# Odd tokens of two batches in one tile, and reciprocals on 128 partitions by way of DRAM, in an attention and gated-MLP kernel for one Trainium2 core

## Chip, core and metric

The kernel runs on one core of a Trainium2 chip. The metric is the device time of one execution in microseconds. Five engines matter: TensorE (PE, matmuls), VectorE (DVE), ScalarE (ACT), GpSimd (POOL) and SyncE (SP), whose queue issues nearly all DMAs.

## What is computed

Four batches of 12 heads, 448 tokens and 64 values a head go through capped attention; the result, 448 tokens by 768, goes through a gated MLP with a residual. In short, from the reference:

```python
scores = cap * np.tanh(scale * np.matmul(q, k.transpose(0, 1, 3, 2)) / cap)
attn = np.exp(scores - np.max(scores, axis=-1, keepdims=True))
attn = attn / (np.sum(attn, axis=-1, keepdims=True) + 1e-09)
x = np.matmul(attn, v)                      # heads side by side: (4, 448, 768)
h = gelu_tanh(x @ w_in)                     # (4, 448, 1024)
u, v = h[..., :512], h[..., 512:]
v_n = (v - mu) / np.sqrt(var + 1e-06) * g_ln
v_s = np.einsum('ts,bsd->btd', w_sg, v_n) + b_sg[None, :, None]
out = x + (u * v_s) @ w_out
```

All inputs are fp32 (`w_in` and `w_out` are float64 words that the kernel decodes itself). To keep the precision, every dense product is made of three matmuls: a value is split into a high part and a rest (both fp32r), and high x high, high x low and low x high are summed in PSUM.

## The kernel before

**Attention.** A batch is 6 pairs of heads, in 3 groups of two pairs. A group has 7 units (L294 to L301): three blocks of 128 keys for each pair, and one unit that holds the odd 64 keys of both pairs. So there are 84 units. A unit is a score product in one of two PSUM tiles `sc` (L533, or L541 for the odd keys, L547 for the very first), a Tanh (L602) and an Exp (L604) of 128 x 896 on ACT into one of six tiles `p`, a product with v into `ps` (L561, L571) and, alone or after a sum on DVE (L621), a product with ones (L478) that adds the row sums into the PSUM bank `den`. DVE or ACT split q and k into `hl` beforehand and copy `ps` into the tiles `x` behind.

**Reciprocals and normalisation.** `recip` (L628) waits for the last L478 of a batch, copies half of `den` (on DVE or ACT), adds the other half and the guard (L631), takes the reciprocals on 64 partitions of 448 (L634) and writes them to DRAM in two DMAs (L637). `norm` (L660) then fetches, for each pair, its two rows spread over 128 partitions (L664, two tiles `n`), multiplies (L667) and splits into `xh` and `xl` (copy, L354). The odd 64 tokens of `xl` also go into columns 448 to 511 of `xh` (L672).

**Gated part.** `gated(b)` has four stages on PE: `hv` (L705, v = x w_in, token tiles of 128 and one of the odd 64 tokens whose other 64 columns hold the low parts), `hu` (L750, u), `vsg` (L767, the product with `w_sg`) and `outp` (L788). Each `hv` and `hu` tile goes through a gelu: ACT (L686), DVE (L688), ACT (L691), DVE (L693). `hv` tiles are then normalised: L724 to L726 on DVE, a power on POOL (L729), L737, and a split. The odd tile has a further copy and addition first (L719, L720), on 64 partitions.

**Order.** Nothing is issued in the order of the text. `Plan` (L128) collects operations with their costs and keys, and `run` (L164) places them on the five queues by a model of the engines: of what is ready first, the lowest key. The keys come from a table of numbers (L23 to L45: `ATT`, `GATED`, `RECIP` and others). The queues themselves are then fixed: each engine works in its order, and an instruction that waits holds all behind it. The odd tile's matmuls in `hv` before are these:

```python
terms = ((0, 0), (0, 1), (1, 0)) if t < FC else ((0, 0), (0, 1))
for c in range(KD):
    ...
            rhs=win[w][:, c, HF:], start=(c == 0 and k == 0),
```

Of the kernel before, what the change touches and what calls it, by code (L numbers as in the profile page):

```python
# [28 lines left out]
SHARED = {'act': 206.9, 'dve': 108.5}
SUMS = (0, 0, 1, 0, 1, 1, 1, 1, 1, 1, 1, 1)  # L30
RETIRE = (12, 9, 12, 12, 12, 0)
IN_V = (95.8, 10.2)
IN_U = (189.1, 37.0)
OUT_W = (-35.4, 5.8)
SG_W = (583.9, 11.2)
FETCH_W = 59.61
FETCH_G = 58.41
SPLIT = 0.0
SG_FETCH = (47.2, 64.6)
GELU = 157.26  # L40
NORM = 236.9
RECIP = 414.62
VAL = 30.18
DEN = 24.2
DEC_AHEAD = 49.6  # L45
# [833 lines left out]
```

## Time and profile before

| | |
|---|---|
| median of 3 runs | 399.18 us (398.41 to 399.54) |
| the profiled execution, its own time | 397.81 us |
| its span, first to last instruction | 396.0 us |
| PE busy | 381.1 us, 96% |
| DVE busy | 301.6 us, 76% |
| ACT busy | 240.1 us, 61% |
| POOL busy | 45.8 us, 12% |
| TensorE clock granted | 1.00 throughout |

Busy time is the time in which at least one instruction of the engine runs. The profiled execution has 1.81 us outside its span and lies 1.37 us under the median. Shares over the whole span hide that DVE and ACT work mostly in the first 280 us: a table by stretches tells more.

### The profile page before, as it was taken

The page shows a single profiled execution, that of the slowest core. Times are in us where ns is not written, and L with a number is a line of the kernel's source. Part 1 is how long each engine was busy: PE and PEld are TensorE (multiplying, and loading weights), DVE is VectorE, ACT ScalarE, POOL GpSimd, SP SyncE. Part 2 cuts the span into 40 slices and gives each one's busy share as a digit, 9 for nine tenths or more (in the row PEclk, how much of TensorE's full clock was granted, in tenths as well). Part 3 has the DMA queues.
Part 4 walks back from the last instruction along what each step waited for, and adds up shares of the span by engine and source line. Part 5 has one row for each costly group of instructions (what it writes and reads, how often), then busy time and mean ns, then how long its engine had stood idle before and what let it go on. Part 6 is the DMA issues. An engine that isn't in the chain of part 4 may idle for free.

```text
span 396.0 us, 5622 instructions
## 1 busy us (share of the span) xinstructions
PE 381.1 (96%) x2118; PEld 254.3 (64%) x2118; DVE 301.6 (76%) x527; ACT 240.1 (61%) x318; POOL 45.8 (12%) x40
## 2 busy tenths in 40 slices
PE   4999999999999999799999999999999999999996
PEld 1343434465458664273564789998488999889995
DVE  3799999899987898888989278575387876387551
ACT  5999999799794489957968744340323532143210
POOL 0244111014231110113110011000001000010000
PEclk9999999999999999999999999999999999999999
DMA  7995454716042136617162000003012002100012
GB/s 250 293 333 160 145 165 117 239 44 187 7 141 71 48 91 188 215 50 228 46 204 102 25 0 0 2 0 116 26 55 93 2 0 94 46 0 2 1 46 93
DMA packets 23690, 38.85 MB, mean 98 GB/s; under 512 B 3248, under 2 KB 21104, under 8 KB 23664
## 3 DMA queue, kind: packets, MB, share of 16 engines
q1 hardware_dynamic: 23520, 38.39, 30.6%
q8 instruction: 16, 0.26, 0.3%
q10 hardware_dynamic: 144, 0.11, 0.1%
q14 instruction: 10, 0.08, 0.1%
HBM read 32.64 MB, written 5.85 MB: 97 GB/s over the span
## 4 chain that ended last, share of the span: by engine, by line
PE 73%; DVE 9%; DMA 8%; POOL 3%; issue 3%; ACT 1%; SPq 1%; DVEq 0%; ACTq 0%; POOLq 0%
PE ps L788 9%; PE ps L561 9%; PE ps L750 8%; PE sc L533 8%; PE ps L705 7%; PE ps L767 7%; PE sc L750 6%; DMA n<-spread 6%; PE sc L788 5%; PE den L478 4%; PE sc L705 4%; PE sc L541 2%; PE sc L767 2%; POOL sm L729 2%; DMA stage<-in_w_out_dram 2%
## 5 line engine op out<-in xcount | busy, mean ns | idle before, releaser
L602 ACT ACTIVATE p<-sc,qsc 128x896 f32<-128x896 f32 x84 | 81.4, 1007 | 17.0 <-PE sc L533 12.2
L604 ACT ACTIVATE p<-p,cap_sb 128x896 f32<-128x896 f32 x84 | 84.2, 1046 | 0.2
L561 PE MATMUL ps<-p,v 128*64 128x448 f32 x288 | 61.2, 553 | 0.6 <-ACT p L604 0.5
L533 PEld LDWEIGHTS sc<-hl 64*128 64x128 f32 x426 | 36.5, 186 | 35.8 <-ACT p L602 21.5
L533 PE MATMUL sc<-hl 64*128 64x448 f32 x426 | 56.9, 390 | 2.2 <-ACT p L602 2.1
L420 POOL TENSOR_TENSOR stage<-stage 128x512 int32<-128x512 int32 (+1 forms) x20 | 32.3, 1618 | 148.2 <-DVE stage L415 143.1
L621 DVE TENSOR_TENSOR p<-p,p 128x896 f32<-128x896 f32 x36 | 39.0, 1089 | 7.1 <-PE ps L561 3.8
L705 PE MATMUL ps<-win,rg 128*128 128x512 f32 x176 | 44.1, 397 | 0.2 <-DVE rg L354 0.2
L788 PE MATMUL ps<-rg,wout 128*128 128x448 f32 x188 | 42.5, 369 | 0.1
L561 PEld LDWEIGHTS ps<-p,v 128*64 128x64 f32 x288 | 17.8, 137 | 37.1 <-issue 25.5
L705 PEld LDWEIGHTS ps<-win,rg 128*128 128x128 f32 x176 | 32.8, 187 | 9.0 <-DVE rg L354 1.4
L788 PEld LDWEIGHTS ps<-rg,wout 128*128 128x128 f32 x188 | 34.9, 188 | 4.6 <-issue 0.6
L750 PE MATMUL ps<-rg,win 128*128 128x448 f32 x166 | 37.1, 367 | 0.7 <-DVE win L354 0.7
L750 PEld LDWEIGHTS ps<-rg,win 128*128 128x128 f32 x166 | 31.1, 188 | 3.9 <-DVE win L354 1.1
L729 POOL TENSOR_TENSOR sm<-sm,pw 128x1 f32<-128x1 f32 (+1 forms) x16 | 13.3, 832 | 166.4 <-DVE sm L726 166.4
L686 ACT ACTIVATE t<-ps 128x448 f32<-128x448 f32 (+1 forms) x18 | 10.2, 566 | 35.2 <-PE ps L705 22.4
L691 ACT ACTIVATE t<-t 128x448 f32<-128x448 f32 (+2 forms) x32 | 19.4, 605 | 18.9 <-DVE t L688 18.9
L767 PE MATMUL ps<-wsg,rg 128*128 128x448 f32 x129 | 29.3, 369 | 0.0
L478 PE MATMUL den<-p,ones_sb 128*32 128x448 f32 x192 | 26.1, 550 | 2.1 <-DVE p L621 2.1
L354 DVE TENSOR_TENSOR hl<-raw,hl 128x896 fp32r<-128x896 f32 (+1 forms) x25 | 27.6, 1107 | 0.6 <-ACT hl L326 0.5
L767 PEld LDWEIGHTS ps<-wsg,rg 128*128 128x128 f32 x129 | 24.1, 188 | 3.6 <-DVE rg L354 0.7
L326 ACT ACTIVATE rg<-u 128x448 fp32r<-128x448 f32 x14 | 8.1, 579 | 27.1 <-DVE u L776 27.1
(106 smaller groups left out, 506.2 us busy)
## 6 DMA issues: line engine op xcount, KB each, us to landing
stage<-in_w_in_dram SPq DMA_DIRECT2D x12, 512.0 KB
raw<-in_q_dram SPq DMA_DIRECT2D x24, 224.0 KB
raw<-in_k_dram SPq DMA_DIRECT2D x24, 224.0 KB
n<-spread SPq DMA_DIRECT2D x24, 224.0 KB
...
```

The lines of the kernel that those rows point to most:

```text
L354: op("dve", c_tt(n), lambda: nc.vector.tensor_tensor(out=out(), in0=a(), in1=b(), op=ALU.subtract), rd=rd, wr=wr, key=key, fast=True)
L420: nc.gpsimd.tensor_tensor(out=a.bitcast(I32), in0=a.bitcast(I32), in1=hi, op=ALU.add)
L478: nc.tensor.matmul(out=den.t[32 * j:32 * j + 32, :S], lhsT=ones_sb[:, kind, NP - 1 - kind - p:NP + 31 - kind - p], rhs=src.t[:, h, :], sta ...
L533: nc.tensor.matmul(out=sc.t[:, h, :S], lhsT=hl[s].t[rows, w, 1, 128 * c - 128:128 * c], rhs=hl[s].t[rows, m, 0], start=(k == 0), stop=(k = ...
L561: nc.tensor.matmul(out=pav[s].t[64 * h:64 * h + 64, :S], lhsT=v[s].t[:, 128 * (c - 1) + 64 * h:128 * (c - 1) + 64 * h + 64], rhs=p.t[:, h, ...
L602: op("act", c_act(2 * S, True, True), lambda p=p, sc=sc: nc.scalar.activation(out=p.t, in_=sc.t[:, :, :S], func=ACTF.Tanh, scale=qsc), rd= ...
L604: op("act", c_act(2 * S, False, True), lambda p=p: nc.scalar.activation(out=p.t, in_=p.t, func=ACTF.Exp, scale=cap_sb), rd=[k_cap], wr=[p] ...
L621: op("dve", c_tt(2 * S), lambda a=a, p=p: nc.vector.tensor_tensor(out=a.t, in0=a.t, in1=p.t, op=ALU.add), rd=[p], wr=[a], key=akey(i) + 5. ...
L705: nc.tensor.matmul(out=ps.t[:, :HF], lhsT=(xl if a else xh)[c].t[:, t * 128:t * 128 + 128], rhs=win[w][:, c, HF:], start=(c == 0 and k == ...
L750: nc.tensor.matmul(out=ps.t[:, :S], lhsT=win[w][:, c, f * 128:(f + 1) * 128], rhs=(xl if a else xh)[c].t[:, :S], start=(c == 0 and k == 0) ...
L767: nc.tensor.matmul(out=ps.t[:, :S], lhsT=(vl if a else vh)[c].t[:, f * 128:(f + 1) * 128], rhs=wsg[w][:, c, :], start=(c == 0 and k == 0), ...
L788: nc.tensor.matmul(out=ps.t[:, :S], lhsT=wout[w][:, f, c * 128:(c + 1) * 128], rhs=(gl if a else gh)[f].t[:, :S], start=(f == 0 and k == 0 ...
```

## The change

1. The odd 64 tokens of batches b and b+1 (b even) share one `hv` tile of 128 tokens with three terms. `hv(3)` is made only in `gated(0)` and `gated(2)`, after `hu`; its second half, `later_v`, is kept in a tile `y` for the next batch. `norm` no longer fills columns 448 to 511; `norm_tails` (L694) fetches the odd tokens' rows of batch b+1 in two DMAs (L699), and for each pair multiplies (L708), copies and subtracts 64 columns. `gated(b)` so needs the attention of b+1 to be finished.
2. `recip` (L632) copies the whole of `den`, writes its four groups of 6 rows to DRAM in four DMAs (L640), reads them back as 128 partitions x 2 x 42 (L643), adds (L646), takes the reciprocal of 42 columns (L649) and writes it to DRAM in four DMAs (L652). `norm`'s fetch (L685) has the same shape as before.
3. All numbers of the order's table are new. The model counts a fetch of `norm` as 2.4 times its bytes, a matmul's overhead as 0.013 instead of 0.016, and the port shared by DVE and POOL differently. The tiles `t` are 4 instead of 3, the tiles `x` 14 instead of 17.

```diff
-ATT = ((24.05, 5.01), (41.39, 4.15), (104.82, 0.41), (135.9, 3.45))
-GATED = ((117.29, 88.64), (248.11, 19.94), (445.31, 9.19), (512.0, 145.13))
-SWITCH = 95.68
-SIZES = (3, 6, 4, 3, 17, 2)
+ATT = ((-7.56, 2.68), (48.49, 1.79), (92.14, 5.46), (-37.59, -1.94))
+GATED = ((148.51, 36.84), (432.7, 24.6), (396.53, 83.56), (473.35, 171.11))
+SWITCH = 321.96
+SIZES = (3, 6, 4, 4, 14, 2)
...
     def recip(b, key):
-        den, t = dens[b], Buf(t_p, cls="r")
-        cop(lambda: t.t[:64, :S], lambda: den.t[64:, :S], S, [den], [t], key - RECIP, True)
-        op("dve", c_tt(S), lambda: nc.vector.scalar_tensor_tensor(
-            out=t.t[:64, :S], in0=t.t[:64, :S], scalar=guard[:64], in1=den.t[:64, :S], op0=ALU.add, op1=ALU.add),
-           rd=[den, k_guard], wr=[t], key=key - RECIP)
-        op("dve", 2.94, lambda: nc.vector.reciprocal(out=t.t[:64, :S], in_=t.t[:64, :S]), wr=[t], key=key - RECIP)
-        rows = Buf(t=spread[b])
-        for h in range(2):
-            op("sp", ISSUE, lambda h=h: nc.sync.dma_start(
-                out=rows.t[h], in_=t.t[32 * h:32 * h + 4 * NP, :S]),
-               rd=[t], wr=[(rows, h)], key=key - RECIP, size=4 * NP * S * 4)
+        den, t, d = dens[b], Buf(t_p, cls="r"), Buf(d_p)
+        sums, rows = Buf(t=dsum[b]), Buf(t=spread[b])
+        key -= RECIP
+        cols = 2 * NP * S // 128
+        cop(lambda: t.t[:, :S], lambda: den.t[:, :S], S, [den], [t], key, True)
+        for j in range(4):
+            op("sp", ISSUE, lambda j=j: nc.sync.dma_start(
+                out=sums.t[j], in_=t.t[32 * j:32 * j + NP, :S]), rd=[t], wr=[(sums, j)], key=key, size=NP * S * 4)
+        n = sums.t[0, 0:1]
+        op("sp", ISSUE, lambda: nc.sync.dma_start(
+            out=d.t, in_=bass.AP(n.tensor, n.offset, [[cols, 128], [2 * NP * S, 2], [1, cols]])),
+           rd=[sums], wr=[d], key=key, size=2 * 128 * 512)
+        op("dve", 0.2, lambda: nc.vector.scalar_tensor_tensor(
+            out=d.t[:, 0], in0=d.t[:, 0], scalar=guard, in1=d.t[:, 1], op0=ALU.add, op1=ALU.add),
+           rd=[k_guard], wr=[d], key=key)
+        op("dve", 0.42, lambda: nc.vector.reciprocal(out=d.t[:, 0], in_=d.t[:, 0]), wr=[d], key=key)
+        m = rows.t[0, 0, 0:1]
+        for k in range(COPIES):
+            op("sp", ISSUE, lambda k=k: nc.sync.dma_start(
+                out=bass.AP(m.tensor, m.offset + k * NP * S, [[COPIES * NP * S, 2], [cols, 64], [1, cols]]), in_=d.t[:, 0]),
+               rd=[d], wr=[(rows, k)], key=key, size=128 * 512)
         return rows
+    recs, later_v = {}, {}
     def gated(b):
         start, span = GATED[b]
         at = [0.0]
         full = 49.5
-        rows = recip(b, akey(NU * NG * (b + 1) - 1))
+        pair = () if b % 2 else (b + 1,)
+        for i in (b, *pair):
+            if i not in recs:
+                recs[i] = recip(i, akey(NU * NG * (i + 1) - 1))
+        rows = recs[b]
...
-            row = rows.t[0, p:p + 1]
+            row = rows.t[0, 0, p:p + 1]
             op("sp", ISSUE, lambda: nc.sync.dma_start(
-                out=rb.t, in_=bass.AP(row.tensor, row.offset, [[4 * NP * S, 2], [NP * S, 4], [0, 16], [1, S]])),
-               rd=[rows], wr=[rb], key=k, size=128 * S * 4)
+                out=rb.t, in_=bass.AP(row.tensor, row.offset, [[NP * S, 2 * COPIES], [0, 64 // COPIES], [1, S]])),
+               rd=[rows], wr=[rb], key=k, size=2.4 * 128 * S * 4)
             op("dve", c_tt(S), lambda: nc.vector.tensor_tensor(
                 out=xr[p].t, in0=xr[p].t, in1=rb.t, op=ALU.mult), rd=[rb], wr=[xr[p]], key=k, fast=True)
             cop(lambda: xh[p].t[:, :S], lambda: xr[p].t, S, [xr[p]], [(xh[p], 0)], k)
             sub(lambda: xl[p].t[:, :S], lambda: xr[p].t, lambda: f32(xh[p].t[:, :S]), S,
-                [xr[p], (xh[p], 0)], [xl[p]], k)
-            op("dve", c_tt(TL), lambda: nc.vector.tensor_tensor(
-                out=xh[p].t[:, S:], in0=xr[p].t[:, S - TL:], in1=f32(xh[p].t[:, S - TL:S]), op=ALU.subtract),
-               rd=[xr[p], (xh[p], 0)], wr=[(xh[p], 1)], key=k)
+                [xr[p], (xh[p], 0)], [(xl[p], 0)], k)
+        def norm_tails(n):
+            tb = Buf(n_p)
+            k = start - NORM
+            for h in range(2):
+                row = recs[n].t[h, 0, 0:1]
+                op("sp", ISSUE, lambda h=h, row=row: nc.sync.dma_start(
+                    out=tb.t[64 * h:64 * h + 64, :NP * TL].rearrange("r (p s) -> r p s", p=NP),
+                    in_=bass.AP(row.tensor, row.offset + S - TL, [[0, 64], [S, NP], [1, TL]])),
+                   rd=[recs[n]], wr=[(tb, h)], key=k, size=64 * NP * TL * 4)
+            for p in range(NP):
+                x = xs[n, p]
+                def y(p=p):
+                    return tb.t[:, TL * p:TL * p + TL]
+                op("dve", c_tt(TL), lambda x=x, y=y: nc.vector.tensor_tensor(
+                    out=y(), in0=x.t[:, S - TL:], in1=y(), op=ALU.mult), rd=[x], wr=[tb], key=k, fast=True)
+                cop(lambda p=p: xh[p].t[:, S:], y, TL, [tb], [(xh[p], 1)], k)
+                sub(lambda p=p: xl[p].t[:, S:], y, lambda p=p: f32(xh[p].t[:, S:]), TL,
+                    [tb, (xh[p], 1)], [(xl[p], 1)], k)
         for p in range(NP):
             norm(p)
+        for n in pair:
+            norm_tails(n)
...
-            terms = ((0, 0), (0, 1), (1, 0)) if t < FC else ((0, 0), (0, 1))
+            regs = (0,) if t < FC else (0, 1)
             for c in range(KD):
                 def fn(c=c):
-                    for k, (a, w) in enumerate(terms):
+                    for k, (a, w) in enumerate(TERMS):
                         nc.tensor.matmul(
                             out=ps.t[:, :HF], lhsT=(xl if a else xh)[c].t[:, t * 128:t * 128 + 128],
-                            rhs=win[w][:, c, HF:], start=(c == 0 and k == 0),
-                            stop=(c == KD - 1 and k == len(terms) - 1))
-                pe(mms(len(terms), HF), fn, [xh[c], xl[c], chunk["in", c, 1]], [ps])
-            n = 128 if t < FC else TL
+                            rhs=win[w][:, c, HF:], start=(c == 0 and k == 0), stop=(c == KD - 1 and k == 2))
+                pe(mms(3, HF), fn, [(x[c], r) for x in (xh, xl) for r in regs] + [chunk["in", c, 1]], [ps])
...
-                cop(vv, lambda: ps.t[n:, :HF], HF, [ps], [v2], key, True)
-                op("dve", c_tt(HF), lambda: nc.vector.tensor_tensor(
-                    out=vv(), in0=vv(), in1=ps.t[:n, :HF], op=ALU.add), rd=[ps], wr=[v2], key=key)
...
+            vh[t], later_v[b + 1] = Buf(r_p), Buf(y_p)
+            for n, h in enumerate((vh[t], later_v[b + 1])):
+                mine, other = slice(TL * n, TL * n + TL), slice(TL - TL * n, 2 * TL - TL * n)
+                cop(lambda h=h, m=mine: h.t[m], lambda m=mine: v2.t[m, :HF], HF, [v2], [(h, 0)], key + 1)
+                sub(lambda h=h, o=other: h.t[o], lambda m=mine: v2.t[m, :HF], lambda h=h, m=mine: f32(h.t[m]), HF,
+                    [v2, (h, 0)], [(h, 1)], key + 1)
...
-        for t in range(NC):
+        if b % 2:
+            vh[FC] = later_v[b]
+        for t in range(FC):
             hv(t)
         for f in range(KF):
             hu(f)
+        if pair:
+            hv(FC)
         for f in range(KF):
```

What the new table moves stands best in the queues. On PE, the rows around the first matmul of `hv` (L705 before, L745 now). Before:

```order
L478 MATMUL den<-p_96,ones_sb 32x448 x2
L478 MATMUL den<-p_94,ones_sb 32x448 x2
L561 MATMUL ps_131<-p_92,v_87 64x448 x2
L561 MATMUL ps_131<-p_97,v_87 64x448 x2
L533 MATMUL sc_129<-hl_85 128x448 x6
L533 MATMUL sc_130<-hl_85 128x448 x6
L705 MATMUL ps_132<-win_63,r_115 128x512
L705 MATMUL ps_132<-win_64,r_115 128x512
```

and now:

```order
L482 MATMUL den<-p_97,ones_sb 32x448 x2
L482 MATMUL den<-p_93,ones_sb 32x448 x2
L482 MATMUL den<-p_94,ones_sb 32x448 x2
L537 MATMUL sc_128<-hl_86 128x448 x6
L537 MATMUL sc_129<-hl_86 128x448 x6
L565 MATMUL ps_130<-p_92,v_87 64x448 x2
L565 MATMUL ps_130<-p_95,v_87 64x448 x2
L565 MATMUL ps_130<-p_96,v_87 64x448 x2
L537 MATMUL sc_128<-hl_86 128x448 x6
L745 MATMUL ps_131<-win_63,r_112 128x512
L745 MATMUL ps_131<-win_64,r_112 128x512
```

Before, 38 score units stand ahead of the first `hv` matmul, and units of the next batch lie between the pieces of `gated(0)`. Now 49 units stand ahead of it, the attention of batches 0 and 1 is complete, and `hv` (54 matmuls), `hu` (72) and the shared odd tile (18) follow with no unit between.

On SP, from the write of the first batch's sums or reciprocals to the first fetch of `norm`. Before:

```order
L637 DMA spread_134<-t_120 24x448 x2
L394 DMA stage_77<-in_w_in_dram 128x512
L513 DMA v_88<-in_vp_dram 128x384
L664 DMA n_123<-spread_134 128x1x448
L664 DMA n_124<-spread_134 128x1x448
```

and now:

```order
L640 DMA dsum_133<-t_117 6x448 x4
L517 DMA v_87<-in_vp_dram 128x384
L643 DMA d_141<-dsum_133 128x2x42
L398 DMA stage_78<-in_w_in_dram 128x512
L590 DMA vt_91<-in_vt_dram 128x128
L652 DMA spread_137<-d_141 2x64x42 x4
L517 DMA v_88<-in_vp_dram 128x384
L398 DMA stage_80<-in_w_in_dram 128x512
L512 DMA raw_84<-in_q_dram 128x448
L512 DMA raw_84<-in_k_dram 128x448
L512 DMA raw_82<-in_q_dram 128x448
L685 DMA n_122<-spread_137 128x1x448
```

Before, one write lies between the sums and the first fetch of `norm`; now a write, a read and a write, and loads of other data are queued behind the waits for each.

On DVE, the first of the odd tokens' products (tile `n`, with `x` of batch 1) in `gated(0)`, which has no counterpart before:

```order
L728 SCALAR_TENSOR_TENSOR t_117<-t_117,ps_132 128x512
L763 TENSOR_SCALAR t_120<-t_120,sm_124 128x512
L410 TENSOR_SCALAR stage_81<-stage_81 128x384
L708 TENSOR_TENSOR n_122<-x_104,n_122 128x64
L733 SCALAR_TENSOR_TENSOR t_118<-t_117,ps_132 128x512
L358 TENSOR_TENSOR rg_575<-n_122,r_112 128x64
L756 BN_STATS sm_125<-t_118 128x6
L708 TENSOR_TENSOR n_122<-x_105,n_122 128x64
```

The gelu of the second `hv` tile (L733) now stands behind an instruction that waits for a fetch from DRAM (L699).

## Rows read from the trace of the kernel before

**Rows 1.** The page's busy time: share of the span, instructions.
```profile
PE 381.1 (96%) x2118; PEld 254.3 (64%) x2118; DVE 301.6 (76%) x527; ACT 240.1 (61%) x318; POOL 45.8 (12%) x40
```

**Rows 2.** Table by stretches of the span (us): busy time of each engine, PE clock, DMA.
```profile
0.00:5.20 5.20, 0.00 (x1) 0.03 (x1) 0.84 (x7) 2.18 (x4) 0.20 (x4) 1.00 0.52 154
5.20:64.70 59.50, 59.50 (x408) 23.57 (x408) 53.82 (x83) 57.46 (x66) 14.64 (x9) 1.00 0.66 213
64.70:92.00 27.30, 26.78 (x158) 13.51 (x158) 25.10 (x47) 24.94 (x33) 3.33 (x3) 1.00 0.53 168
92.00:124.10 32.10, 30.50 (x180) 18.59 (x177) 28.39 (x52) 26.35 (x34) 8.89 (x5) 1.00 0.31 92
124.10:160.00 35.90, 35.20 (x209) 21.44 (x209) 30.74 (x52) 25.61 (x34) 4.87 (x4) 1.00 0.37 105
160.00:200.00 40.00, 37.04 (x223) 20.44 (x222) 35.86 (x59) 32.75 (x40) 6.30 (x3) 1.00 0.45 139
200.00:392.20 192.20, 192.09 (x953) 156.70 (x952) 126.18 (x233) 70.81 (x111) 7.59 (x13) 1.00 0.13 43
392.20:396.00 3.80, 0.00 (x0) 0.00 (x0) 0.65 (x2) 0.00 (x0) 0.00 (x0) 1.00 0.19 60
```

**Rows 3.** Chain that ended last, PE's pieces: start us, us, what.
```profile
11.47 1.42 PE sc L533 x11
...
14.69 0.79 PE sc L533 x6
...
223.22 4.20 PE ps L705 x18
```

**Rows 4.** PE's timeline in a late attention stretch: start us, us, instructions, idle before.
```profile
167.40 0.96 PE L478 MATMUL den<-p,ones_sb 128*32 128x448 f32 x8 [1.52 <-DVE p L621]
186.54 0.88 PE L533 MATMUL sc<-hl 64*128 64x448 f32 x6 [0.82 <-ACT p L602]
```

**Rows 5.** Timeline of the start, SP's queue, ACT and PE.
```profile
0.74 0.38 SPq L341 DMA_DIRECT2D cap_sb<-in_cap_dram  x1
1.18 0.42 SPq L508 DMA_DIRECT2D raw<-in_q_dram  x1
5.20 1.87 PE L547 MATMUL sc<-raw 64*128 64x448 f32 x4 [5.20 <-DMA raw<-in_k_dram]
7.10 1.01 ACT L602 ACTIVATE p<-sc,qsc 128x896 f32<-128x896 f32 x1 [1.44 <-PE sc L547]
```

**Rows 6.** ACT's timeline, first attention stretch: pairs of Tanh, four units from row to row.
```profile
46.38 1.91 ACT L602 ACTIVATE p<-sc,qsc 128x896 f32<-128x896 f32 x2
...
53.68 1.93 ACT L602 ACTIVATE p<-sc,qsc 128x896 f32<-128x896 f32 x2
```

**Rows 7.** DVE's groups by line and shape: count, busy us, mean ns, idle before.
```profile
L634 DVE RECIPROCAL t<-t 64x448 f32<-64x448 f32 x4 | 11.8, 2938 | 0.0
L720 DVE TENSOR_TENSOR t<-t,ps 64x512 f32<-64x512 f32 x4 | 2.7, 665 | 0.0
L324 DVE COPY x<-ps 128x448 f32<-128x448 f32 x13 | 8.0, 614 | 0.8 <-PE ps L571 0.4 <-PE ps L561 0.4
L672 DVE TENSOR_TENSOR rg<-x,rg 128x64 fp32r<-128x64 f32 x22 | 4.7, 216 | 0.0
L667 DVE TENSOR_TENSOR x<-x,n 128x448 f32<-128x448 f32 x24 | 15.8, 667 | 6.2 <-DMA n<-spread 6.0
```

**Rows 8.** Timeline around batch 0's reciprocals, SP's queue and DVE.
```profile
63.02 0.74 SPq L637 DMA_DIRECT2D spread<-t  x2
65.22 1.33 SPq L664 DMA_DIRECT2D n<-spread  x2
71.09 0.60 SPq L664 DMA_DIRECT2D n<-spread  x1
77.00 0.62 DVE L667 TENSOR_TENSOR x<-x,n 128x448 f32<-128x448 f32 x1 [0.38 <-DMA n<-spread]
```

**Rows 9.** DVE's timeline: the gelu of `gated(0)`'s first `hu` tile ends.
```profile
123.48 0.62 DVE L693 SCALAR_TENSOR_TENSOR u<-t,ps 128x448 f32<-128x448 f32 x1 [0.64 <-ACT t L691]
```

More of the change, by code (lines that the diff above doesn't have):

```diff
@@ L20 @@
 TERMS = ((0, 0), (0, 1), (1, 0))
-ATT = ((24.05, 5.01), (41.39, 4.15), (104.82, 0.41), (135.9, 3.45))
-GATED = ((117.29, 88.64), (248.11, 19.94), (445.31, 9.19), (512.0, 145.13))
-SWITCH = 95.68
-SIZES = (3, 6, 4, 3, 17, 2)
+ATT = ((-7.56, 2.68), (48.49, 1.79), (92.14, 5.46), (-37.59, -1.94))
+GATED = ((148.51, 36.84), (432.7, 24.6), (396.53, 83.56), (473.35, 171.11))
+SWITCH = 321.96
+SIZES = (3, 6, 4, 4, 14, 2)
 RS = 19
+COPIES = 4
 G_CAP = 2
[L29 to L45, printed above, removed]
+SHARED = {'act': 77.0, 'dve': 202.1}
+SUMS = (0, 1, 1, 0, 1, 0, 1, 1, 1, 1, 1, 1)
+RETIRE = (10, 12, 9, 10, 0, 2)
+IN_V = (156.1, 36.0)
+IN_U = (111.9, 73.9)
+OUT_W = (180.7, 8.8)
+SG_W = (1132.9, 26.5)
+FETCH_W = 186.16
+FETCH_G = 1.55
+SPLIT = 5.25
+SG_FETCH = (375.2, 62.2)
+GELU = 150.5
+NORM = 148.13
+RECIP = 371.46
+VAL = 46.92
+DEN = 45.31
+DEC_AHEAD = 116.5
 ISSUE = 0.45
@@ L85, in __init__ @@
     def __init__(self, tiles, caps=None):
-        self.free = [(0.0, i, t) for i, t in enumerate(tiles)]
+        self.free = [(-1.0, i, t) for i, t in enumerate(tiles)]
         self.n = len(tiles)
@@ L184, in run @@
                     if o.fast and e in port:
-                        t = max(t, port["dve" if e == "pool" else "pool"])
+                        t = max(t, port["dve"] + 0.14 if e == "pool" else port["pool"])
                     if o.alloc:
@@ L308 @@
     t_p = Pool(tiles(TS, [128, 512], FP32, "t"))
+    y_p = Pool(tiles(1, [128, 512], FP32R, "y"))
     n_p = Pool(tiles(NS, [128, S], FP32, "n"))
@@ L312 @@
     ps_p = Pool([pp.tile([128, 512], FP32, name=f"ps{i}") for i in range(3)], {"g": G_CAP, "b": 2})
-    spread = [dp.tile([2, 4 * NP, S], FP32, name=f"spread{b}") for b in range(B)]
+    dsum = [dp.tile([4, NP, S], FP32, name=f"dsum{b}") for b in range(B)]
+    spread = [dp.tile([2, COPIES, NP, S], FP32, name=f"spread{b}") for b in range(B)]
+    d_p = Pool(tiles(1, [128, 2, 2 * NP * S // 128], FP32, "d"))
     den_p = Pool([pp.tile([128, 512], FP32, name="den")])
@@ L333, in mms @@
     def mms(n, cols=None, sets=None, records=None):
-        return n * (cols or S) / 2400.0 + 0.016 * (sets or n) + 0.0059 * (records or n)
+        return n * (cols or S) / 2400.0 + 0.013 * (sets or n) + 0.0059 * (records or n)
     k_cap, k_ones, k_bsg, k_g, k_pw = (Buf() for _ in range(5))
@@ L714, in vv @@
             def vv():
[L715 to L722 removed]
+                return v2.t[:, :HF]
@@ L732, in hv @@
+            op("dve", 0.55, lambda: nc.vector.tensor_scalar(
+                out=vv(), in0=vv(), scalar1=sm.t[:, 6:7], scalar2=sm.t[:, 0:1],
+                op0=ALU.subtract, op1=ALU.mult), rd=[sm], wr=[v2], key=key + 1)
             if t < FC:
-                vl[t] = Buf(r_p)
-            def lo():
-                return vl[t].t if t < FC else vh[t].t[n:]
-            op("dve", 0.55, lambda: nc.vector.tensor_scalar(
-                out=vv(), in0=vv(), scalar1=sm.t[:n, 6:7], scalar2=sm.t[:n, 0:1],
-                op0=ALU.subtract, op1=ALU.mult), rd=[sm], wr=[v2], key=key + 1)
@@ L740, in hv @@
-            cop(lambda: vh[t].t[:n], vv, HF, [v2], [(vh[t], 0)], key + 1)
-            sub(lo, vv, lambda: f32(vh[t].t[:n]), HF, [v2, (vh[t], 0)], [vl[t] if t < FC else (vh[t], 1)], key + 1)
+                h, lo = vh[t], vl[t] = Buf(r_p), Buf(r_p)
+                cop(lambda: h.t, vv, HF, [v2], [h], key + 1)
+                sub(lambda: lo.t, vv, lambda: f32(h.t), HF, [v2, h], [lo], key + 1)
+                return
+            vh[t], later_v[b + 1] = Buf(r_p), Buf(y_p)
[4 more added lines that the diff above has]
+                    [v2, (h, 0)], [(h, 1)], key + 1)
```

17 lines of the change are left out of this document (6 added, 11 removed).

## The prediction

> **What bounds the kernel now.** I read the page's busy time first, then a table by stretches, then the chain and the timelines at the places where PE waits. PE is busy 96% of the span, every other engine 76% or less [rows 1]. The table says where the other 4% lies [rows 2]: 5.20 us ahead of the first matmul, 3.80 us behind the last, and between them 0.52, 1.60, 0.70 and 2.96 us in the four stretches from 64.7 to 200 us, together 5.78 us. From 5.2 to 64.7 us, and again from 200 us on, PE shows practically no idle time. So the time is PE's work, plus the start, the end and some 6 us of waits. The clock column stands at 1.00 throughout, so the clock plays no part.
>
> The second thing to see is who is nearly full beside PE. Up to 124.1 us DVE works 0.84 + 53.82 + 25.10 + 28.39 = 108.2 us, nine tenths of the time [rows 2]; ACT works 57.46 of 59.50 us in the first attention stretch. PE's waits are on these two: 1.52 us on DVE's sum of two `p`, 0.82 us on a Tanh [rows 4]. After 200 us both have room.
>
> **PE's work.** `hv` had 3 x 18 + 12 = 66 matmuls of 512 columns a batch, 264 in all. Now an even batch has 4 x 18 = 72 and an odd one 54: 252. Eighteen of them took 4.20 us on the chain [rows 3], 0.2333 us each, so 12 fewer are **-2.80 us**. The other counts are equal: 72 whole score and value units with 12 odd ones, 26 passes for the sums, and the same `hu`, `vsg` and `outp`. Changes between kinds of matmul are 131 before and 132 now, by the two orders; a score unit that stands alone takes 0.79 us and two in a row 1.42 us (one of their twelve records is missing) [rows 3], so one more change is **+0.1 us**.
>
> **The start.** q of the first pair is now issued ahead of `cap`, 1.18 - 0.74 = 0.44 us earlier, so PE starts at about 4.75 us instead of 5.20 [rows 5]. ACT gets the split of a whole pair before its first Tanh, which so comes at about 7.1 us, as now, and the second Tanh is followed by both Exps: PE waits some 0.2 us more there. Net **-0.2 us**. The end has the same last additions and stores: 0.
>
> **Attention first.** 49 units (38 before) now precede `hv`. PE's work for them, priced kind by kind from the chain, with the start, puts the first `hv` matmul at about 99 us. ACT does four units in 53.68 - 46.38 = 7.30 us, 1.825 us each [rows 6]: 49 x 1.825 = 89.4 us and some 2.5 us of copies, from 7.1 to 99 us. Both are full, as they were in the first stretch, where PE showed no wait. I take **0.5 us** of wait.
>
> **DVE in the gated part.** From `hv` on DVE is what counts, because the order puts both decodes and the gelu of three stages there. Take the end of the first `hu` tile's gelu, without which PE cannot begin the third `hu` tile. Before, it is DVE's 184th instruction and ends at 124.1 us [rows 9] with 108.2 us of work done. Now it is the 202nd. The difference by kinds: three more copies of `ps` (0.614 each, 1.8), ten operations on 64 columns instead of six (0.216 each, 0.9), the decode of two and a half chunks of `w_out` and some casts that ACT had before (about 7.3), two reciprocals of 42 columns with their additions and a copy (about 1.8); less 2.94 and some 0.7 for the old reciprocal, less seven instructions of a half tile of `hv` (3.6, L720 among them), less two splits of `hv` tiles that now come later (1.8) [rows 7]. That is 2.8 us more, 111.0 us. DVE starts at about 3.5 us. At the last split of q and k ahead of `hv` it must wait until PE has finished with that `hl` buffer, at about 92.3 us by PE's sum, with only some 82 us of work behind it: it will have idled 7 us by then. So it comes to that gelu's end at 3.5 + 111.0 + 7.0 = 121.5 us. PE, by its own work, wants it at 119.4 us. That is 2.1 us of wait, plus whatever else DVE idles in these 27 us; from 64.7 to 124.1 us it idled 59.4 - 53.5 = 5.9 us [rows 2], but most of that was room that PE did not need. I take **3.0 us** in all, and the later `vsg` and `outp` tiles to 165 us follow DVE at its own pace.
>
> **Attention of the last two batches.** Between two pieces of `outp` 24 units stand on PE in about 44 us; ACT needs 24 x 1.825 = 43.8 us [rows 6]. Balanced: **1.0 us**. Behind it come `gated(2)` and `gated(3)`, where nothing waited before: 0.
>
> **The moved DMAs.** `recip` now issues nine DMAs a batch instead of two, and a pair of batches two more for the odd tokens; SP has 40 such issues where it had 8, of 0.37 us each [rows 8], spread over 300 us: nothing by themselves. What counts is the chain: sums out, in, reciprocals out, rows in. Its steps are not in this trace. The nearest rows bound one step: a small write had landed before the fetch behind it was issued, 65.22 - 63.76 = 1.5 us at most, and a fetch of 224 KB released DVE 77.00 - 71.09 = 5.9 us after its issue [rows 8]. I take 2.3 us, near the small write, since the new pieces are small, too. For batch 0 some 40 us lie between the last sums and `hv`. For batch 1 the last sums are done at about 95.7 us; a copy (0.6), issues, an addition and a reciprocal (4.5 with the copy and its wait) and four steps put the odd tokens' rows at 96 + 4.5 + 9.2 = about 110 us. DVE comes to the first L708 at about 112 us by the sum above. So it hides, barely; the cover is DVE's own lateness. Behind that L708 stands the gelu of the second `hv` tile (L733), and PE's next tile in that `ps` bank waits for it.
>
> The Trainium skill ("DMA: Bandwidth & Descriptors", Specifications) speaks against this part: below 512 bytes a piece, a DMA does read-modify-write, and the new pieces are 168 and 256 bytes. No row here shows such a piece by itself; by the rule a step would move from 2.3 us toward the upper bound, and the sum by what the slower rival below says.
>
> **Sum.** Waits between start and end: 0.5 + 3.0 + 1.0 = 4.5 instead of 5.78, -1.3 us. With -2.8, +0.1 and -0.2: -4.2 us. The profiled execution's 397.81 us becomes 393.6; the median lies 1.37 us above it, so the forecast is **395.0 us**. About 0.3%, 1.2 us, is what a measurement of this kernel can tell from no change: faster is below 398.0, slower above 400.4.
>
> **Rivals.**
> - *DVE idles as long as it does now.* To the first `hu` tile's gelu it idled 124.1 - 3.5 - 108.2 = 12.4 us. With 111.0 us of work the point comes at 126.9, 7.5 us after PE wants it; waits of 0.5 + 7.5 + 1.0 = 9.0 us are 3.2 more than now and undo the -2.9 of the rest: **399.5 us**, no change. For it: two PE waits on DVE now are where it is less full. Against: the part of its idling that PE forces falls from some 11 to 7 us, as DVE has work there.
> - *The odd tokens' rows come late.* At 5.9 us a step they land at 96 + 4.5 + 23.6 = 124 us, and DVE stands at the first L708 for 12 us with the gelu behind it; PE fills both its `ps` banks and stops. Waits of 12 + 1.5 = 13.5, 7.7 more than now: 399.18 - 2.9 + 7.7 = **404.0 us**. It begins to cost at (112 - 100.5) / 4 = 2.9 us a step and turns the change into a loss when L708 waits 8.4 us, at 5.0 us a step. For it: the steps follow each other, and all three DVE waits for DRAM rows are in its order. Against: the small write [rows 8] is well under. In batches 2 and 3 it costs nothing: 34 us lie between the last sums and that tile.
> - *The new order hides nearly all waits.* Waits of 0.5 us: 399.18 - 2.9 - 5.3 = **391.0 us**. For it: twelve PE waits of under 1.6 us each are small things that an order can cover. Against: the sum for DVE above.
> - That the matmuls do not go is excluded: both orders show their numbers, and PE is the bound where they stand.
>
> The same page of the Trainium skill ("DMA: Bandwidth & Descriptors", Anatomy of one DMA — SWDGE (gpsimd) path) names about 2.0 us as the fixed cost of a DMA on another issue path. By that figure four steps take 8 us, and the late rival does not occur; the rows above allow it and do not settle it.
>
> **How the numbers follow.** Forecast 0.60, no change by DVE 0.15, slower by the rows 0.10, hidden waits 0.15. Faster 0.60 + 0.15 = 0.75, same 0.15, slower 0.10. The range takes in the forecast, the DVE rival and the hidden waits, and leaves out the late rows: 391.0 to 399.8 us.
>
> **What would show it.** PE busy near 378.5 us, with 252 `hv` matmuls. First matmul at 4.7 to 4.8 us, first `hv` at 98 to 100 us. Between 92 and 165 us DVE busy over 93%, and PE's waits there released by DVE, 2 to 4 us in all. L708 without a wait of over 1 us on its fetch; a long one there says that the second rival holds. From 214 to 260 us ACT over 95% busy. The prediction is wrong if PE's work falls by less than 2.5 us, or if waits of more than 8 us stand between the first and the last matmul.

## The result, and the profile after

The changed kernel takes **393.53 us** (median of four runs, 392.94 to 395.32) against 399.04 us before: a ratio of 0.987, 95% interval 0.983 to 0.991. In a second comparison (experiment 5), with six runs against 17 of the kernel before, the ratio was 0.992 (0.990 to 0.994). So it is faster by 0.8 to 1.3%; the forecast of 395.0 us with a range of 391.0 to 399.8, which also takes in no change, held. The profiled execution took 393.91 us, 3.90 less than the one before, with a span of 392.1 us.

The page's busy time after the change, answering to [rows 1]:

```profile
PE 379.7 (97%) x2106; PEld 253.7 (65%) x2106; DVE 290.3 (74%) x519; ACT 233.3 (59%) x314; POOL 48.5 (12%) x38
```

The table by stretches, with the columns and, but for the moved start and end, the stretches of [rows 2]:

```profile
0.00:4.01 4.01, 0.00 (x1) 0.03 (x1) 0.09 (x2) 1.92 (x3) 0.21 (x4) 1.00 0.43 120
4.01:64.70 60.69, 60.54 (x400) 23.70 (x404) 55.93 (x98) 57.58 (x65) 21.84 (x8) 1.00 0.66 223
64.70:92.00 27.30, 25.48 (x176) 10.22 (x170) 26.00 (x42) 23.69 (x28) 5.09 (x3) 1.00 0.63 174
92.00:124.10 32.10, 30.29 (x151) 21.39 (x148) 28.66 (x65) 22.16 (x36) 6.03 (x6) 0.95 0.40 114
124.10:160.00 35.90, 35.58 (x196) 25.80 (x195) 33.61 (x64) 24.56 (x39) 8.18 (x6) 1.00 0.43 126
160.00:200.00 40.00, 40.00 (x189) 34.97 (x188) 25.40 (x47) 14.88 (x25) 3.00 (x4) 1.00 0.10 35
200.00:388.20 188.20, 187.80 (x1008) 137.61 (x1006) 119.97 (x207) 88.46 (x123) 4.15 (x7) 1.00 0.18 59
388.20:392.10 3.90, 0.00 (x0) 0.00 (x0) 0.67 (x2) 0.00 (x0) 0.00 (x0) 1.00 0.18 59
```

PE idles 4.01 us ahead of the first matmul, 3.90 behind the last, and 0.15 + 1.82 + 1.81 + 0.32 + 0 + 0.40 = 4.5 us between them; before it was 5.20, 3.80 and 5.9. New is a clock of 0.95 in the fourth stretch. What PE waited for, from the view of its waits (us in total, times, longest):

```profile
PE sc L551 <- DMA raw<-in_k_dram: 4.0, 1, 4.0
PE den L482 <- DVE p L625: 1.8, 2, 1.0
PE ps L785 <- DVE t L733: 1.8, 1, 1.8
PE ps L823 <- DVE rg L358: 0.4, 1, 0.4
PE ps L565 <- ACT p L608: 0.3, 1, 0.3
```

The waits on a Tanh (2.1 us in all before, the 0.82 of [rows 4] among them) are gone. The new one is PE's third: before the first `hu` tile, for the gelu of the second `hv` tile. DVE's timeline at that place:

```profile
113.33 0.36 DVE L410 TENSOR_SCALAR stage<-stage 128x384 f32<-128x384 f32 x1 [1.10 <-DMA stage<-in_w_out_dram]
114.51 0.22 DVE L708 TENSOR_TENSOR n<-x,n 128x64 f32<-128x64 f32 x1 [0.82 <-DMA n<-spread]
114.72 0.69 DVE L733 SCALAR_TENSOR_TENSOR t<-t,ps 128x512 f32<-128x512 f32 x1
```

and PE's, followed by three of the windows behind it:

```profile
115.46 0.47 PE L785 MATMUL ps<-r,win 128*128 128x448 f32 x1 [1.81 <-DVE t L733]
```

```profile
116.00:118.00 2.00, 2.00 (x7) 1.79 (x6) 2.00 (x9) 0.77 (x4) 1.25 (x2) 0.50 0.01 4
116.00:120.00 4.00, 4.00 (x14) 3.57 (x13) 4.00 (x13) 1.97 (x6) 1.79 (x2) 0.58 0.01 2
120.00:124.00 4.00, 4.00 (x21) 3.68 (x20) 3.17 (x12) 1.42 (x4) 0.55 (x1) 1.00 0.02 4
```

DVE stands for a fetch twice, 1.92 us, with L733 behind it. PE stood 1.81 us, and then the granted clock was 0.50 (1.2 GHz) from 116 to 118 us and 1.00 (2.4 GHz) from 120 us on: the first `hu` tile took 115.46 to 120.78 = 5.32 us, the next one 124.46 - 120.78 = 3.68 us.

The chain that led there stands in SP's queue (start us, us, instruction):

```profile
97.00 1.30 SPq L640 DMA_DIRECT2D dsum<-t  x4
...
100.63 0.38 SPq L643 DMA_DIRECT2D d<-dsum  x1
105.79 2.30 SPq L652 DMA_DIRECT2D spread<-d  x4
108.13 1.03 SPq L398 DMA_DIRECT2D stage<-in_w_out_dram  x1
109.27 1.32 SPq L699 DMA_DIRECT2D n<-spread  x2
```

Not all of the chain is DRAM. SP waits for the read of the sums twice (us in total, times, longest); the longest is this one, from 101.08 to 104.13 us, so the read took 3.5 us from its issue at 100.63:

```profile
SPq L652 <- DMA d<-dsum: 4.5, 2, 3.1
```

The addition that needs the sums then stands behind VectorE's other work, without an idle moment, until 105.06 us:

```profile
104.52 0.61 DVE L358 TENSOR_TENSOR wsg<-u,wsg 128x448 fp32r<-128x448 f32 x1
105.06 0.25 DVE L646 SCALAR_TENSOR_TENSOR d<-d,guard 128x42 f32<-128x42 f32 x1
```

### The profile page after: what moved, and what is told of

Read it like the earlier page. It is cut to its first block, busy times and chain, and to the rows that moved or that the text cites. A ratio compares the mean times of both kernels' runs of the same rounds, so it can differ in the third digit from the quotient of the medians.

```text
span 392.1 us, 5650 instructions
## 1 busy us (share of the span) xinstructions
PE 379.7 (97%) x2106; PEld 253.7 (65%) x2106; DVE 290.3 (74%) x519; ACT 233.3 (59%) x314; POOL 48.5 (12%) x38
## 4 chain that ended last, share of the span: by engine, by line
PE 78%; DVE 10%; DMA 6%; ACT 2%; SPq 2%; issue 1%; DVEq 0%
PE ps L823 12%; PE ps L785 12%; PE ps L565 10%; PE sc L537 9%; PE ps L745 9%; PE ps L802 7%; PE den L482 4%; PE sc L785 4%; PE sc L745 3%; PE sc L823 3%; DMA n<-spread 3%; PE ps L575 2%; PE sc L802 2%; DVE p L625 2%; DVE hl L358 1%
## 5 line engine op out<-in xcount | busy, mean ns | idle before, releaser
L537 PE MATMUL sc<-hl 64*128 64x448 f32 x426 | 56.5, 387 | 0.1
L424 POOL TENSOR_TENSOR stage<-stage 128x512 int32<-128x512 int32 (+1 forms) x20 | 39.3, 1968 | 107.3 <-DVE stage L419 93.8
L823 PE MATMUL ps<-rg,wout 128*128 128x448 f32 x208 | 48.4, 369 | 0.4 <-DVE rg L358 0.4
L785 PE MATMUL ps<-rg,win 128*128 128x448 f32 x206 | 45.8, 375 | 0.0
L745 PE MATMUL ps<-win,rg 128*128 128x512 f32 x188 | 45.1, 395 | 0.0
L625 DVE TENSOR_TENSOR p<-p,p 128x896 f32<-128x896 f32 x36 | 40.2, 1118 | 5.0 <-PE ps L565 2.8
L785 PEld LDWEIGHTS ps<-rg,win 128*128 128x128 f32 x206 | 39.9, 194 | 3.8
L823 PEld LDWEIGHTS ps<-rg,wout 128*128 128x128 f32 x208 | 38.6, 188 | 5.3 <-issue 0.9
L745 PEld LDWEIGHTS ps<-win,rg 128*128 128x128 f32 x188 | 35.2, 187 | 8.5
L761 POOL TENSOR_TENSOR sm<-sm,pw 128x1 f32<-128x1 f32 x14 | 9.0, 645 | 198.3 <-DVE sm L758 198.3
L358 DVE TENSOR_TENSOR hl<-raw,hl 128x896 fp32r<-128x896 f32 (+1 forms) x25 | 27.2, 1090 | 5.7 <-ACT hl L330 5.5
L731 ACT ACTIVATE t<-t 128x448 f32<-128x448 f32 (+1 forms) x30 | 18.1, 604 | 17.9 <-DVE t L728 17.9
L728 DVE SCALAR_TENSOR_TENSOR t<-t,ps 128x448 f32<-128x448 f32 (+1 forms) x23 | 14.9, 648 | 15.8 <-ACT t L726 15.8
L802 PE MATMUL ps<-wsg,rg 128*128 128x448 f32 x112 | 25.9, 368 | 0.0
L802 PEld LDWEIGHTS ps<-wsg,rg 128*128 128x128 f32 x112 | 20.9, 188 | 2.9 <-issue 0.7
```

Of the source, the lines that this page charges most:

```text
L358: op("dve", c_tt(n), lambda: nc.vector.tensor_tensor(out=out(), in0=a(), in1=b(), op=ALU.subtract), rd=rd, wr=wr, key=key, fast=True)
L424: nc.gpsimd.tensor_tensor(out=a.bitcast(I32), in0=a.bitcast(I32), in1=hi, op=ALU.add)
L537: nc.tensor.matmul(out=sc.t[:, h, :S], lhsT=hl[s].t[rows, w, 1, 128 * c - 128:128 * c], rhs=hl[s].t[rows, m, 0], start=(k == 0), stop=(k = ...
L625: op("dve", c_tt(2 * S), lambda a=a, p=p: nc.vector.tensor_tensor(out=a.t, in0=a.t, in1=p.t, op=ALU.add), rd=[p], wr=[a], key=akey(i) + 5. ...
L745: nc.tensor.matmul(out=ps.t[:, :HF], lhsT=(xl if a else xh)[c].t[:, t * 128:t * 128 + 128], rhs=win[w][:, c, HF:], start=(c == 0 and k == ...
L785: nc.tensor.matmul(out=ps.t[:, :S], lhsT=win[w][:, c, f * 128:(f + 1) * 128], rhs=(xl if a else xh)[c].t[:, :S], start=(c == 0 and k == 0) ...
```

## Experiments

In the expectations, 393.5 us is the changed kernel's time in the first comparison. Ratios are to the kernel before on the same chip. Kernels with lines added show L733, L785 and others 7 or 8 higher.

**1. Put the matmuls back.**

```diff
-                    for k, (a, w) in enumerate(TERMS):
+                    for k, (a, w) in [(9, TERMS[0])] * (2 * (b % 2) * (c == 0)) + list(enumerate(TERMS)):
```

(with start and stop set for k = 9, so that each extra product is a group of its own)

> The changed kernel with 12 hv matmuls of 512 columns put back (six each in batches 1 and 3, a first product made three times, so that the output stays the same); the order of everything else is unchanged. If TensorE's work bounds the time, each costs 0.2333 us as in the trace: +2.80 us, 396.3 us against the changed kernel's 393.5. If the gain came from the order and the waits and TensorE has room, 393.5 us and no change; a value near 395 would say that half of the work hides in waits.

Measured: 396.52 us, ratio 0.998 (0.996 to 1.000). The profiled span is 394.5 us, against 392.1 and 392.0 us in the two profiles of the changed kernel: +2.5 us, of 2.80 expected; against the 0.992 (0.990 to 0.994) of experiment 5 the ratio gives as much, 0.6%. TensorE's work is on the path. With it put back the kernel is within 0.4% of the kernel before, so what the order and the reciprocals add to it is small.

**2 and 3. Load VectorE, there and elsewhere.** In the first tile of batch 0, then of batch 2:

```diff
-            op("dve", 0.69, lambda: nc.vector.bn_stats(out=sm.t[:, 0:6], in_=vv()), rd=[v2], wr=[sm], key=key + 1)
+            op("dve", 0.69, lambda: [nc.vector.bn_stats(out=sm.t[:, 0:6], in_=vv()) for _ in range(5 if b == 0 and t == 0 else 1)], rd=[v2], wr=[sm], key=key + 1)
```

> The changed kernel with the statistics (L756) of the first hv tile of batch 0 made five times instead of once: four more at 0.61 us, 2.4 us of VectorE work at 110 us of the span, same output, same order. Theory of the prediction: VectorE's work sets when the gelu of the second hv tile (L733) ends, so the wait of 1.81 us before the first hu matmul grows by 2.4 us, 395.9 us or, if the clock falls longer behind it, up to 398. Rival: VectorE's fetches set it (it stood 1.10 us before L410 and 0.82 us before L708 for DMAs), the work fits into these 1.92 us, the wait grows by 0.5 us, 394.0 us.

> The same four extra statistics in the first hv tile of batch 2 instead, behind 262 us, where VectorE is busy 63% of the time and TensorE showed no wait. Both theories: the time stays, 393.5 us, and TensorE's waits stay 4.3 us in all. If it grows by 2.4 us as well, VectorE's chain is on the path there too, and the prediction was wrong to call the last third covered.

Measured: 394.77 us, ratio 0.992 (0.990 to 0.995), and 394.98 us, ratio 0.992 (0.989 to 0.995). PE's timeline with the work at 110 us:

```profile
116.32 0.74 PE L785 MATMUL ps<-r,win 128*128 128x448 f32 x1 [2.93 <-DVE t L733]
```

and VectorE's, with the five statistics:

```profile
109.26 3.60 DVE L756 BATCH_NORM_STATS2 sm<-t 128x6 f32<-128x512 f32 x5
```

They took 3.60 us instead of the 0.68 of one, so 2.9 us of work were added, more than the 2.4 expected. VectorE's two stands for fetches are gone there: 2.9 us of work replaced 1.92 us of waiting, and PE's wait grew by 1.1 us, about the difference. The median is within the noise of the same work in batch 2, whose profiled execution has a new PE wait of 0.78 us at 319 us (`vsg`, for L358). So at that place the fetches, more than VectorE's work, set the time; the last third seems nearly, not quite, covered.

**4. The gelu ahead of the fetches.** The order of everything else is kept; two VectorE operations, by their numbers in the plan, and what follows from them are held until L733 is issued:

```diff
+HELD, UNTIL = (128, 508), 552
...
-            fn()
+            if o.num in HELD or any(o in h.succ for h, _ in held):
+                held.append((o, fn))
+            else:
+                fn()
+            if o.num == UNTIL:
+                while held:
+                    held.pop(0)[1]()
```

> The changed kernel with one VectorE instruction moved two places forward: the gelu's last product of the second hv tile (L733) stands ahead of L410 and L708, which wait for DMAs. Its input from ScalarE is there at 112.3 us. If these waits hold TensorE, the wait of 1.81 us before the first hu matmul goes and the granted clock stays at 1.00 behind it (1.64 us): -1.8 to -3.4 us, less what the third hv tile's gelu then makes the second hu tile wait, some 1 to 1.5 us: 391 to 393 us. If VectorE's work is the limit, the wait only moves to the next tile: 393.5 us, with 1.8 us of wait before the second or third hu tile.

Measured: 393.76 us, ratio 0.989 (0.985 to 0.993). PE's only wait between 74 and 143 us:

```profile
117.35 0.47 PE L792 MATMUL ps<-r,win 128*128 128x448 f32 x1 [1.31 <-DVE t L740]
```

The wait before the first `hu` tile is gone and the second tile (here L792) has 1.31 us of the 1.81. The profiled execution took 390.58 us, with its fetches some 2 us earlier than in the changed kernel's profile (L708 stood 0.31 us, at 112.3 us); the other five took 393.2 to 395.8. The waits are as forecast for the theory, but most of the first is handed to the next tile; the time is a miss, since 393.76 us is the rival's 393.5 and the ratio is not shown to be under the 0.992 (0.990 to 0.994) of experiment 5.

**5. The changed kernel again**, as the yardstick for the rest.

> The changed kernel once more, unchanged, as the yardstick on the chip of this group: a ratio to the kernel before of 0.987, as measured, that is 4 to 5.5 us less. All theories expect the same.

Measured: 394.53 us, ratio 0.992 (0.990 to 0.994). The same wait stands at the same place, but the clock behind it does not fall:

```profile
116.23 0.47 PE L785 MATMUL ps<-r,win 128*128 128x448 f32 x1 [1.95 <-DVE t L733]
```

```profile
116.00:120.00 4.00, 3.77 (x18) 3.30 (x18) 4.00 (x13) 2.59 (x7) 1.79 (x2) 1.00 0.05 19
```

**6. The odd tokens later still** (the edit is against experiment 4).

```diff
-HELD, UNTIL = (128, 508), 552
+HELD, UNTIL = (128, 508), 569
```

> The changed kernel with L410 and the first three odd-token products (L708) and what follows from them held back until the gelu of the third hv tile (its L733) has been issued. The earlier run with only the second hv tile's L733 ahead showed the wait again at the second hu tile, 1.3 us. If instructions that wait for fetches hold TensorE here, both waits go: no wait of over 0.5 us between 112 and 124 us, 1.8 us of wait and 1.6 us of clock less than the changed kernel, 2 to 3.5 us. Rival: VectorE's work comes due elsewhere, a later hu or hv tile waits as long, and the time equals the changed kernel's within 1 us.

Measured: 396.30 us, ratio 0.996 (0.994 to 0.998). In this kernel one chunk of `w_out` is decoded from words that the next step has already changed, since L419 was not held with L410, so its output is wrong; the amount of work is the same. The profiled execution, 399.19 us, is the slowest of the twelve. In it the first `hu` tile's wait is gone, but the second waits 2.5 and the third 2.7 us: ScalarE stood 1.64 us at its own decode of the next chunk, with the third tile's Square behind it. A miss: three instructions on two engines wait for fetches here, and I had moved those of one engine.

**7. All three behind.** Held by operation: L410 and its followers until the second tile's L733, the odd tokens until the third tile's, ScalarE's L406 until its Square. The line replaces that of experiment 4, and the loop keeps a mark for each held operation.

```diff
+HELD = {128: 552, 508: 569, 135: 566}
```

> The changed kernel with what waits for fetches moved behind what TensorE needs, on VectorE and ScalarE alone: the second hv tile's L733 ahead of L410, the odd tokens' products (L708) behind the third hv tile's L733, and ScalarE's decode of the next w_out chunk (L406) behind the third tile's Square (L726). If these three waits hold TensorE, no wait of over 0.5 us is left between 112 and 124 us and the time is 1.5 to 3.5 us under the changed kernel: ratio to the kernel before 0.983 to 0.988. Rival: VectorE has no slack in the stretch, the odd tokens' work of some 4.5 us then stands ahead of the first hu tiles' gelu, a later hu tile waits 1.5 to 3 us, and the ratio stays at 0.99.

Measured: 393.54 us, ratio 0.989 (0.986 to 0.991).

```profile
117.63 0.47 PE L793 MATMUL ps<-r,win 128*128 128x448 f32 x1 [0.23 <-DVE t L741]
123.17 0.47 PE L793 MATMUL ps<-r,win 128*128 128x448 f32 x1 [1.62 <-DVE u L741]
```

The first wait goes, the second shrinks to 0.23 us, and the third tile waits 1.62 us, since the odd tokens' work now stands ahead of its gelu. The rival came out: the fetches caused the stand at the first tile, but PE's waits still add up to 1.85 us, so VectorE has little to give in this stretch. The median is 1.0 us under that of experiment 5; the two intervals overlap, so it is not shown to beat the changed kernel.

**8. `cap` on another queue**, on top of 7.

```diff
-    load(lambda: cap_sb, cap.partition_broadcast(128), k_cap, 512, -98.7)
+    op("sp", ISSUE, lambda: nc.scalar.dma_start(out=cap_sb, in_=cap.partition_broadcast(128)), wr=[k_cap], key=-98.7, size=512)
```

> The same, and cap is loaded by ScalarE's queue instead of SyncE's, so that q and k of the second pair are issued 0.47 us earlier. The trace of the changed kernel shows the second unit's product (L545) held until their k lands at 7.4 us. If that hold is on the path, 0.4 to 0.5 us less than the run before it; rival: ScalarE's own attention work bounds the first 65 us, and nothing is gained.

Measured: 393.59 us, ratio 0.989 (0.987 to 0.991): nothing gained. PE's start in the changed kernel, and then here:

```profile
4.01 1.86 PE L551 MATMUL sc<-raw 64*128 64x448 f32 x4 [4.01 <-DMA raw<-in_k_dram]
5.80 3.42 PE L545 MATMUL sc<-raw 64*64 64x448 f32 x8
9.31 1.88 PE L537 MATMUL sc<-hl 64*128 64x448 f32 x12
```

```profile
5.63 1.87 PE L559 MATMUL sc<-raw 64*128 64x448 f32 x4 [5.63 <-DMA raw<-in_k_dram]
7.43 1.77 PE L553 MATMUL sc<-raw 64*64 64x448 f32 x8
9.13 2.25 PE L545 MATMUL sc<-hl 64*128 64x448 f32 x12
```

The hold inside the second unit is gone (1.77 us instead of 3.42), but the first k, issued at 1.19 us in both, landed 1.6 us later. The third unit begins at 9.13 instead of 9.31 us.

**9 to 12. Parts alone**, each with the order planned anew.

> The changed kernel with the reciprocals of the kernel before (2.94 us of VectorE a batch on 64 partitions, one DRAM write instead of write, read, write), order planned anew with the same numbers. If the added DRAM steps are what makes the odd tokens late, L708 no longer waits and the stall before the first hu tile shrinks: 1 to 3 us faster than the changed kernel. If VectorE's work is the limit between 92 and 165 us, its 1.7 us more a batch come out as 1.5 to 3.5 us of wait: 395 to 397 us. The order is planned again, which can add 1 us either way.

> The changed kernel with the old table of numbers (15 tiles x and 3 tiles t, so that it fits), so with attention and gated part interleaved as before, 38 units ahead of hv; shared odd tile and DRAM reciprocals stay. By my account the twelve matmuls are worth 2.8 us wherever they stand, and order and start together about 1 us: some 2 to 3 us faster than the kernel before, ratio 0.992 to 0.995. Rival: the gain is the new order's; then this kernel is as the one before or slower, ratio 1.0 or over, with waits of 8 us or more because the shared tile makes batch 0 wait for batch 1's attention.

> The kernel before with the new reciprocals alone (old order numbers, 16 tiles x so that it fits, 264 hv matmuls, order planned anew). VectorE loses 1.7 us of work a batch, the rows come three DRAM steps later, some 10 us, and norm's fetches wait for them. By my account TensorE is the bound and the waits are small: within 1% of the kernel before, 0.995 to 1.005. Rival: the reciprocals carry the gain, 0.990.

> The kernel before with the new order numbers and model alone (sizes of the pools included; 264 hv matmuls, old reciprocals). By my account it has 2.8 us more matmul work than the changed kernel with the old reciprocals, which measured 1.008: 1.01 to 1.02, slower than the kernel before, since the numbers were fitted to other code. Rival: attention first is a gain by itself, 0.993.

| kernel | shared odd tile | reciprocals | order numbers | us | ratio (95%) |
|---|---|---|---|---|---|
| changed (experiment 5) | yes | new | new | 394.53 | 0.992 (0.990 to 0.994) |
| 9. old reciprocals | yes | old | new | 401.17 | 1.008 (1.006 to 1.011) |
| 10. old numbers | yes | new | old | 424.09 | 1.067 (1.064 to 1.069) |
| 11. reciprocals alone | no | new | old | 407.48 | 1.025 (1.022 to 1.029) |
| 12. numbers alone | no | old | new | 416.96 | 1.047 (1.045 to 1.050) |

The edits are the change's own pieces: in 9 and 11 the `recip` of the other kernel with its `spread` and the fetch of `norm`; in 10 and 12 the table of the other kernel, in 12 with the model but for the factor on `norm`'s fetch (10 with 15 tiles `x`, 11 with 16, so that they fit).

Four misses of mine, though 10 went the rival's way: each part alone, or the whole without one, is slower than the kernel before, up to 26 us. How it comes about shows best in 11, one row each of VectorE, ScalarE and TensorE:

```profile
161.92 0.62 DVE L679 TENSOR_TENSOR x<-x,n 128x448 f32<-128x448 f32 x1 [3.10 <-DMA n<-spread]
```

```profile
162.58 0.58 ACT L329 ACTIVATE rg<-x 128x448 fp32r<-128x448 f32 x1 [3.12 <-DVE x L679]
```

```profile
165.03 1.78 PE L536 MATMUL sc<-hl 64*128 64x448 f32 x12 [2.51 <-ACT p L605]
```

VectorE waits for the rows from DRAM, ScalarE's copy waits for VectorE, the Tanh behind the copy is late, and PE waits for the Tanh: with the old numbers there is no room for the added steps. In 10 the largest wait is a `vsg` tile's, for the split of the shared odd tile. That tile's last matmul ends at 170.19 us, and its split (L358) comes 12 us later; 1.90 us of this VectorE stands for rows from DRAM in a product of `norm` (L688) put ahead of it, as VectorE's and PE's rows show:

```profile
181.60 0.63 DVE L688 TENSOR_TENSOR x<-x,n 128x448 f32<-128x448 f32 x1 [1.90 <-DMA n<-spread]
182.26 0.69 DVE L358 TENSOR_TENSOR rg<-t,rg 64x512 fp32r<-64x512 f32 x1
```

```profile
183.00 1.11 PE L802 MATMUL ps<-wsg,rg 128*128 128x448 f32 x2 [6.64 <-DVE rg L358]
```

In 9 TensorE's waits are spread over seven sources behind the first matmul, 3.5 us of them on Tanhs. How much of its 6.6 us over experiment 5 is VectorE's 1.7 us more a batch, and how much an order that was fitted to other operations, is not settled: every one of these kernels has another order.

## Why the prediction was right, and where not

- **TensorE's work, -2.8 us: right.** The trace has 252 `hv` matmuls, and experiment 1 gives 2.5 us in the span. Busy time fell by only 1.4 us instead of 2.6, my own sign for a wrong prediction; 1.64 us of the first `hu` tile at a lower clock count as busy in this execution. The second profile, at full clock, has PE at 378.4 us, the forecast 378.5. That this agrees so well is luck: in both profiles some 1.7 us of standing inside L545 (3.42 us, and twice 1.76 us, instead of 1.77) count as busy, and less standing elsewhere made up for it.
- **The waits, 4.5 us: right in sum by luck, wrong in parts.** I put 0.5 us in the attention, 3.0 on VectorE in the gated part and 1.0 on ScalarE between the `outp` pieces. Measured: 1.8 on the sums of `p` (L625) between 64.7 and 92 us, 1.8 before the first `hu` tile, 0.3 and 0.4 later, nothing between 214 and 260 us, where ScalarE was busy 36.06 of 46 us instead of the 95% I had named as a sign. The estimate of 1.825 us a unit of [rows 6] is not what bounds that stretch. Against the third rival I had counted twelve short waits before; there were eleven.
- **The reason for VectorE's lateness: half wrong.** I summed its work and let the DRAM steps hide under it, "barely". It reached the first L708 at 113.7 us (forecast 112) because L410 had held it for 1.10 us, and there it stood 0.82 us more. With these stands moved (experiments 4 and 7) 1.3 to 1.9 us of wait came back at the next tiles, where VectorE stood for a fetch no longer than 0.31 us. It was busy 67.09 of 73 us between 92 and 165, 92%; I had said over 93%.
- **The step that was mis-sized: 2.3 us for a DRAM step.** The chain began with the copy at 96.43 us, as forecast (95.7 to 96), and released L708 at 114.51: 18.1 us for 13.7. The writes kept to the price, as far as the next issue tells: the sums' read was issued 2.3 us after the last issue of their write, and the odd tokens' rows 1.2 us after the last of the reciprocals'. The reads did not: the sums took 3.5 us, the rows 5.2 (109.27 to 114.51). That is at most 12.2 us for the four steps, 3.1 each, and 1.03 of it SP's issue of a `w_out` load that the order put ahead of L699. The other 5.8 us, for 4.5, are the engines': 3.6 for SP's issues of the eight writes, 0.9 in which L646 stood behind VectorE's own work, and the rest for the copy, the addition and the reciprocal. Put on the steps alone, as in the prediction, the lateness is (114.5 - 100.5) / 4 = 3.5 us a step, past the 2.9 us from which the late-rows rival was to cost, and short of the 5.0 at which it turns the change into a loss: the mechanism of that rival happened, but L708 stood for 0.82 us instead of 12. The other 1.10 us in front of L733 are L410's, which waited for a `w_out` load, and no rival had that.

  The nearest row for a read was the 5.9 us fetch of [rows 8], and I had taken a value near the write for both. The Trainium skill ("DMA: Bandwidth & Descriptors", Anatomy of one DMA — SWDGE (gpsimd) path), with its fixed 2.0 us, comes out low for these two reads. Its rule on pieces below 512 bytes (same page, Specifications) is not what made the sums' read long: in batch 3 the same read, in the same pieces of 168 bytes, took 1.8 us (issued at 280.35, SP's wait for it over at 282.2), behind one store; in batch 1 it stood behind two loads (98.99 and 100.09). For the rows the cause stays open: a `w_out` load, in pieces of 3 KB, took as long (108.13 to L410 at 113.33 us), but it is twice the bytes, and both were issued behind the writes of the reciprocals.
- **The start, -0.2 us: wrong sign.** PE began at 4.01 us, earlier than the 4.75 forecast, but L545 then had to wait for the second pair's k. Only the first pair's loads had moved ahead of `cap`; the second k was issued when it had been before, in this row of before and this of after:

```profile
2.59 0.43 SPq L508 DMA_DIRECT2D raw<-in_k_dram  x1
```

```profile
2.60 0.43 SPq L512 DMA_DIRECT2D raw<-in_k_dram  x1
```

The third unit began at 9.31 us against 8.69 before, +0.6 us; before, the second unit had run without a hold:

```profile
6.99 1.77 PE L541 MATMUL sc<-raw 64*64 64x448 f32 x8
8.69 1.49 PE L533 MATMUL sc<-hl 64*128 64x448 f32 x6
```

I had followed the first pair's loads past `cap` and not asked when the second's come.

- **What made up for it.** The 2.1 us of waits on Tanhs before went entirely, and PE also stood less inside pieces that count as busy: from the start of each score matmul to that of the next instruction, summed over its 426 records, it is 56.5 us before and 53.2 after, 3.3 less. Of these 2.5 were shown as waits before (1.52 for a sum, 0.82 for a Tanh, 0.20 for an Exp). I had no term for the other 0.8.

The sum of -4.2 us (profile: -3.9) so came out of one right large term and several small ones that missed on both sides and happened to cancel. Had each DRAM step come out 1.5 us dearer still, the change would have been a loss by the working of the prediction.
